# The second feed-forward matmul by Strassen's algorithm (seven half-block products for eight) in a fused hash-attention and feed-forward kernel

## The chip, the cores and the metric

One core of a Trainium2 chip. The metric is the device time of one execution in microseconds (us), smaller is better; it is quoted as the median of several executions, with the lowest and the highest. "Span" is the time that the profile of one execution shows; it is some 2 us less than the device time.

## The reference

```python
mask = q_bucket[:, :, :, None] == k_bucket[:, :, None, :]   # buckets from the signs of q @ proj, k @ proj (6 bits)
scores = np.where(mask, scale * q @ k.T, -1e9)
attn = softmax(scores)                                       # cut: with max and + 1e-9
x = (attn @ v)                                               # to (3072, 512)
h = x @ w_in                                                 # (3072, 2048)
g = h * (1 / (1 + exp(-h)))
out = g @ w_out                                              # (3072, 512)
```

Four batches of eight heads, 768 positions, 64 elements a head. A batch of attention yields 768 rows for the feed-forward part.

## The kernel before

The kernel goes through 288 steps, nine per head and 72 per batch. A step has one score matmul of 512 columns (two of 256 in every third step), one exp on ScalarE and four attention matmuls. Two heads are a "pair". While batch b is scored, TensorE works off "units" of the feed-forward part of batch b - 1, laid between the steps; a unit is 0.87 us of TensorE. What is left runs after the last score. Other work is planned by hand at fixed steps: the transposes of q and k (VectorE, L246), their casts (GpSimd, L251), the projection that yields the hash bits (L281), the loads.

The parts that the change touches; `ps` is the pool in PSUM. The tag "m" has three buffers, shared by h, the output sums, the projections and the transposes:

```python
        def mm1(ci, grp, dts=slice(0, NDT)):
            ... # cut
            hp = ps.tile([P, f, n], F32, tag="m", name="h_ps", bufs=3)
            ... # cut: 4 or 8 matmuls into hp (L461), tanh on ScalarE into th (L468)
            after.append(lambda: nc.vector.scalar_tensor_tensor(        # L470, frees hp
                out=g[ci][:, grp * f : (grp + 1) * f, :], in0=th, scalar=1.0, in1=hp,
                op0=ALU.add, op1=ALU.mult))

        def mm2(tt, part):
            ci, ct = (0, tt) if tt < 4 else (1, tt - 4)
            if part == 0:
                tag = "m" if scoring else "s"
                o2[tt] = ps.tile([P, DMODEL], F32, tag=tag, name="o2_ps", bufs=3)
            for ft in range(4 * part, 4 * part + 4):
                nc.tensor.matmul(o2[tt], g[ci][:, ft, ct * P : (ct + 1) * P],   # L496
                                 w_out16[:, ft, :],
                                 start=(ft == 0), stop=(ft == NFT - 1))
            if part == 3:
                ... # cut: eviction on VectorE (L501), output transfer
```

A row tile's sum takes four units of four matmuls and is then evicted once. Six row tiles a batch.

The softmax here doesn't subtract the row's maximum and nothing guards it: scores larger than these inputs give would overflow.

## Time and profile before

| | before |
|---|---|
| time, median of 3 | 303.24 us (303.05 to 303.79) |
| span of the profiled run | 301.3 us |
| granted TensorE clock | 1.0 |
| second matmul | 384 matmuls of 512 columns or their like |

The most telling views are in the prediction below. First VectorE's row in the 40 slices (each 7.5 us; a digit is the busy share in tenths): it has free time in most slices.

```profile
DVE  5797938899588355854694434954443443664332
```

Second, two stretches of steps (columns: from and to in us, length, then busy us and count of TensorE, weight loads, VectorE, ScalarE, GpSimd; then the clock, the DMA share and GB/s). The first is steps 96 to 126, the second steps 186 to 198:

```profile
69.60:94.00 24.40, 24.32 (x248) 15.54 (x246) 19.32 (x32) 20.78 (x40) 11.71 (x21) 1.00 0.99 168
148.20:159.20 11.00, 11.00 (x106) 6.93 (x105) 10.41 (x14) 8.70 (x17) 5.29 (x5) 1.00 0.60 107
```

TensorE fills both. In the second VectorE is already busy 10.41 of 11.00 us: there is no room there, and this was in plain sight before the change.

### The profile page before, as it was taken

The page shows a single profiled execution, that of the slowest core. Times are in us where ns is not written, and L with a number is a line of the kernel's source. Part 1 is how long each engine was busy: PE and PEld are TensorE (multiplying, and loading weights), DVE is VectorE, ACT ScalarE, POOL GpSimd, SP SyncE. Part 2 cuts the span into 40 slices and gives each one's busy share as a digit, 9 for nine tenths or more (in the row PEclk, how much of TensorE's full clock was granted, in tenths as well). Part 3 has the DMA queues.
Part 4 walks back from the last instruction along what each step waited for, and adds up shares of the span by engine and source line. Part 5 has one row for each costly group of instructions (what it writes and reads, how often), then busy time and mean ns, then how long its engine had stood idle before and what let it go on. Part 6 is the DMA issues. An engine that isn't in the chain of part 4 may idle for free.

```text
span 301.3 us, 7181 instructions
## 1 busy us (share of the span) xinstructions
PE 296.6 (98%) x2710; PEld 175.1 (58%) x2710; DVE 180.1 (60%) x344; ACT 210.1 (70%) x392; POOL 128.3 (43%) x203
## 2 busy tenths in 40 slices
PE   8999999999999999999999999999999999999996
PEld 3676855545665665555565665555566654446653
DVE  5797938899588355854694434954443443664332
ACT  5987989989886777778876666978977722452200
POOL 7589999388418551935158401755111100000000
PEclk9999999999999999999999999999999999999999
DMA  7999997999988638834078135011022003001112
GB/s 202 243 237 199 181 153 115 199 212 173 150 187 145 107 102 211 126 84 133 3 139 133 49 74 189 2 42 31 2 61 63 20 21 93 35 2 70 37 68 71
DMA packets 103170, 32.87 MB, mean 109 GB/s; under 512 B 90656, under 2 KB 100192, under 8 KB 103136
## 3 DMA queue, kind: packets, MB, share of 16 engines
q1 hardware_dynamic: 98752, 28.22, 44.6%
q0 software_dynamic: 4224, 4.19, 9.0%
q8 instruction: 21, 0.34, 0.5%
q14 instruction: 13, 0.11, 0.1%
q10 hardware_dynamic: 160, 0.00, 0.0%
HBM read 27.27 MB, written 6.29 MB: 111 GB/s over the span
## 4 chain that ended last, share of the span: by engine, by line
PE 88%; DVE 7%; DMA 1%; ACT 1%; issue 1%; SPq 1%; DVEq 0%; ACTq 0%
PE o_ps L496 26%; PE h_ps L461 24%; PE s_ps L366 19%; PE o_ps L398 12%; DVE g L470 3%; PE bp_ps L281 3%; PE tp_ps L185 2%; DMA k_row<-in_k_dram 1%; PE o_ps L482 1%; DVE qk L246 1%; DVE qka L343 1%; ACT u L369 1%; DVE osum L412 1%; SPq L79 0%; PE o_ps L389 0%
## 5 line engine op out<-in xcount | busy, mean ns | idle before, releaser
L369 ACT ACTIVATE u<-s_ps 128x512 f16<-128x512 f32 x288 | 157.0, 606 | 38.7 <-PE s_ps L366 38.3
L470 DVE SCALAR_TENSOR_TENSOR g<-th,h_ps 128x512 f16<-128x512 f32 x96 | 65.5, 687 | 73.8 <-ACT th L468 73.8
L461 PE MATMUL h_ps<-xT,win 128*128 128x512 f16 (+1 forms) x512 | 98.4, 325 | 0.1
L398 PEld LDWEIGHTS <-u 128*128 128x128 f16 x1152 | 68.1, 98 | 42.2 <-ACT u L369 8.4
L496 PE MATMUL o_ps<-wout,g 128*128 128x512 f16 x368 | 91.6, 379 | 0.0
L398 PE MATMUL o_ps<-vv,u 128*128 128x65 f16 x1152 | 82.6, 194 | 0.5 <-ACT u L369 0.4
L468 ACT ACTIVATE th<-h_ps 128x512 f32<-128x512 f32 x96 | 57.9, 603 | 35.9 <-PE h_ps L461 33.2
L461 PEld LDWEIGHTS <-win 128*128 128x128 f16 x512 | 49.9, 98 | 30.5 <-issue 0.4
L418 POOL TENSOR_TENSOR x_pr<-osum,rec 128x384 f16<-128x384 f32 x23 | 19.0, 826 | 88.5 <-DVE rec L417 88.0
L496 PEld LDWEIGHTS <-g 128*128 128x128 f16 x368 | 35.8, 98 | 33.7
L366 PE MATMUL s_ps<-qka 71*128 71x512 f16 x192 | 52.7, 327 | 0.0
L366 PE MATMUL s_ps<-qkb 128*128 128x512 f16 x192 | 52.6, 326 | 0.0
L251 POOL TENSOR_SCALAR qka<-qk 64x1536 f16<-64x1536 f32 x15 | 22.0, 1466 | 11.5 <-DVE qk L246 5.7
L501 DVE TENSOR_SCALAR osb<-o_ps 128x512 f32<-128x512 f32 x23 | 15.9, 691 | 15.0 <-PE o_ps L496 15.0
L251 POOL TENSOR_SCALAR qkb<-qk 64x1536 f16<-64x1536 f32 x15 | 22.1, 1471 | 1.2
L262 POOL TENSOR_TENSOR vsa<-v_sb 128x192 f32<-128x192 f32 x32 | 18.9, 591 | 0.0
L260 POOL CAST vv<-v_sb 128x384 f16<-128x384 f32 x32 | 16.2, 507 | 1.0 <-DMA v_sb<-in_v_dram 0.6
L246 DVE STREAM_TRANSPOSE qk<-k_blk 128x768 f32<-128x768 f32 x10 | 15.8, 1582 | 0.3 <-issue 0.3
L246 DVE STREAM_TRANSPOSE qk<-q_blk 128x768 f32<-128x768 f32 x10 | 16.0, 1596 | 0.0
L366 PEld LDWEIGHTS <-qka 71*128 71x128 f16 x192 | 15.5, 97 | 0.4 <-ACT qka L238 0.3
L366 PEld LDWEIGHTS <-qkb 128*128 128x128 f16 x192 | 15.4, 97 | 0.0
L412 DVE TENSOR_TENSOR osum<-o_ps,vsum 128x390 f32<-128x390 f32 x23 | 13.0, 565 | 2.3
(70 smaller groups left out, 162.5 us busy)
## 6 DMA issues: line engine op xcount, KB each, us to landing
out_dram<-osb SPq DMA_DIRECT2D x23, 256.0 KB
v_sb<-in_v_dram SPq DMA_DIRECT2D x15, 384.0 KB
q_blk<-in_q_dram SPq DMA_DIRECT2D x40, 96.0 KB
k_blk<-in_k_dram SPq DMA_DIRECT2D x40, 96.0 KB
win<-in_moe_w_in_dram POOLq DMA_DIRECT2D x4, 512.0 KB, 7.7
wout<-in_moe_w_out_dram POOLq DMA_DIRECT2D x4, 512.0 KB, 6.2
q_sb<-in_q_dram SPq DMA_DIRECT2D x5, 384.0 KB
k_sb<-in_k_dram SPq DMA_DIRECT2D x5, 384.0 KB
```

What stands on the lines that cost most here:

```text
L246: nc.vector.transpose(out=dst, in_=qk_sb[p, "qk"[n]])
L251: nc.gpsimd.tensor_scalar(out=dst[rows, :], in0=qk32[p][rows, :], scalar1=CS, scalar2=1.0, op0=ALU.mult, op1=ALU.mult)
L260: nc.gpsimd.tensor_copy(out=vv[:, :, 0:D], in_=src)
L262: nc.gpsimd.tensor_tensor(out=sa, in0=src[:, 0:3], in1=src[:, 3:6], op=ALU.add)
L366: nc.tensor.matmul(sp[:, o0 : o0 + n], t[rows, S + jt * P : S + (jt + 1) * P], t[rows, c0 : c0 + n], start=True, stop=True)
L369: nc.scalar.activation(out=u, in_=sp, func=AF.Exp, scale=ESC)
L398: nc.tensor.matmul(o_ps[h][:, c0 // P + i, :], u[:, o0 + i * P : o0 + (i + 1) * P], vv[:, jt, :], start=(not direct(h) and w % NU == 0 and ...
L418: (nc.vector if direct(h) else nc.gpsimd).tensor_tensor(out=x_pr[p][:, :, par * D : (par + 1) * D], in0=o[:, 0:NJ, 0:D], in1=rec[:, :, Non ...
L461: nc.tensor.matmul(hp[:, j, :], w_in16[:, dt, ft * P : (ft + 1) * P], xT[4 * b + dt][:, c0 : c0 + n], start=(dt == 0), stop=(dt == NDT - 1))
L468: nc.scalar.activation(out=th, in_=hp, func=AF.Tanh, scale=0.5)
L470: after.append(lambda: nc.vector.scalar_tensor_tensor(out=g[ci][:, grp * f : (grp + 1) * f, :], in0=th, scalar=1.0, in1=hp, op0=ALU.add, o ...
L496: nc.tensor.matmul(o2[tt], g[ci][:, ft, ct * P : (ct + 1) * P], w_out16[:, ft, :], start=(ft == 0), stop=(ft == NFT - 1))
```

## The change

Intent: TensorE is the bound, so multiply less. The matrix product of one chunk of rows is cut into 2 x 2 blocks and done by Strassen's algorithm in Winograd's form, with seven block products for eight. The seven share PSUM sums so that few extra additions are needed. VectorE makes the combinations of the blocks of g (for each chunk) and of w_out (once), in float16. The core of the diff:

```diff
-    ld = ...bufs=4  vld = ...bufs=4  t32 = ...bufs=3          # shortened here: three pools
+    ld = ...bufs=3  vld = ...bufs=3  t32 = ...bufs=2
+    def w_unit(n, half):                                       # planned at steps 96 to 110, 1024 elements each
+        f = slice(half * NK // 2, (half + 1) * NK // 2)
+        dst, x, y = {1: (wt[1], B12, B11), 2: (wt[2], B22, wt[1]),
+                     3: (B12, B22, B12), 4: (wt[4], B21, wt[2])}[n]
+        nc.vector.tensor_tensor(out=dst[:, f], in0=x[:, f], in1=y[:, f], op=ALU.subtract)
...
-        def mm2(tt, part):                                     # and mm2_last: removed
+        def comb(ci, n, f):                                    # cut: choice of blocks
+            nc.vector.tensor_tensor(out=dst, in0=x, in1=y, op=op)
...
+        def product(ci, n, t):
+            nt = 2 - ci
+            bank, x, y = {1: (1, (0, 0), B11), 2: (1, (1, 0), B21),
+                          6: (2, (0, 0), wt[2]), 5: (2, (0, 1), wt[1]), 3: (2, (1, 0), B22),
+                          7: (3, None, B12), 4: (3, (1, 1), wt[4])}[n]
+            ... # cut: a product opens its bank for n in 1, 6, 7
+            for k in range(NK):
+                nc.tensor.matmul(op[:, t, :], x[:, k, t * P : (t + 1) * P], y[:, k],
+                                 start=(first and k == 0), stop=True, skip_group_check=True)
+            ... # cut
+            add = {1: None, 2: None, 6: 1, 5: 1, 3: 1, 7: 5, 4: 6}[n]
+            keep = n in (1, 6, 5)                              # a copy in the middle of a sum
+            ... # cut: eviction of op, plus kept[add], scaled by 0.5; output transfer unless keep
...
+        units = spread(first[:-3], late) if late else first[:-3]
+        units = units + [big[0]] + first[-3:] + [big[1]] + spread(second, big[2:8])
+        late[:] = big[8:] + small
...
-            skip = w * 36 // 66 == (w - 1) * 36 // 66
+            skip = w * 32 // 66 == (w - 1) * 32 // 66
...
+    last += [late[i] for i in (6, 0, 1, 7, 8, 2, 3, 9, 4, 10, 11, 5, 12)]
```

Line numbers in the changed kernel: L474 first matmul, L524 product, L378 score, L410 attention matmul, L293 projection, L486 g, L507 combination of g, L186 combination of w_out, L534 eviction, L536 eviction with an addition, L258 block transpose of q and k, L263 cast.

More of the change, by code (lines that the diff above doesn't have):

```diff
@@ L47 @@
     cst = ctx.enter_context(tc.tile_pool(name="cst", bufs=1))
-    ld = ctx.enter_context(tc.tile_pool(name="ld", bufs=4))
-    vld = ctx.enter_context(tc.tile_pool(name="vld", bufs=4))
-    t32 = ctx.enter_context(tc.tile_pool(name="t32", bufs=3))
+    ld = ctx.enter_context(tc.tile_pool(name="ld", bufs=3))
+    vld = ctx.enter_context(tc.tile_pool(name="vld", bufs=3))
+    t32 = ctx.enter_context(tc.tile_pool(name="t32", bufs=2))
     btp = ctx.enter_context(tc.tile_pool(name="btp", bufs=2))
@@ L163 @@
     w_out16 = cst.tile([P, NFT, DMODEL], F16, name="wout")
+    NK = NFT // 2
+    NC = DMODEL // 2
+    wt = {n: cst.tile([P, NK, NC], F16, name=f"wt{n}") for n in (1, 2, 4)}
+    B11, B12 = w_out16[:, 0:NK, 0:NC], w_out16[:, 0:NK, NC:DMODEL]
+    B21, B22 = w_out16[:, NK:NFT, 0:NC], w_out16[:, NK:NFT, NC:DMODEL]
     def load_w_in(i):
@@ L444, in moe_units @@
     def moe_units(b):
-        g = {}
+        blk = {}
         opened = {}
@@ L451, in mm1 @@
             c0, n, f = ((0, 512, 1), (512, 256, 2))[ci]
-            if ci not in g:
-                g[ci] = gpl.tile([P, NFT, n], F16, tag=f"g{ci}", name="g",
-                                 bufs=2 - ci)
+            ft0 = grp * f
+            half = ft0 // NK
+            if (ci, half) not in blk:
+                blk[ci, half] = gpl.tile([P, 2, NK, n // 2], F16, tag=f"g{ci}{half}", name="g",
+                                         bufs=2 if (ci, half) == (0, 1) else 1)
             hp = opened.pop((ci, grp), None)
             if dts.start == 0:
-                hp = ps.tile([P, f, n], F32, tag="m", name="h_ps", bufs=3)
+                hp = ps.tile([P, 2, f, n // 2], F32, tag="m", name="h_ps", bufs=3)
             for j in range(f):
-                ft = grp * f + j
+                ft = ft0 + j
                 for dt in range(dts.start, dts.stop):
-                    nc.tensor.matmul(hp[:, j, :], w_in16[:, dt, ft * P : (ft + 1) * P],
-                                     xT[4 * b + dt][:, c0 : c0 + n],
+                    nc.tensor.matmul(hp[:, :, j, :], w_in16[:, dt, ft * P : (ft + 1) * P],
+                                     xT[4 * b + dt][:, c0 : c0 + n]
+                                     .rearrange("d (r c) -> d r c", r=2),
                                      start=(dt == 0), stop=(dt == NDT - 1))
@@ L466, in mm1 @@
                 return
-            th = thp.tile([P, f, n], F32, tag="th", name="th")
+            th = thp.tile([P, 2, f, n // 2], F32, tag="th", name="th")
             nc.scalar.activation(out=th, in_=hp, func=AF.Tanh, scale=0.5)
-            after.append(lambda: nc.vector.scalar_tensor_tensor(
-                out=g[ci][:, grp * f : (grp + 1) * f, :], in0=th, scalar=1.0, in1=hp,
-                op0=ALU.add, op1=ALU.mult))
-        o2 = {}
-        def mm2_last():
-            for c in (slice(0, 384), slice(384, DMODEL)):
-                n = c.stop - c.start
-                op = ps.tile([P, n], F32, tag="s", name="o2_ps", bufs=3)
-                for ft in range(NFT):
-                    nc.tensor.matmul(op, g[1][:, ft, P : 2 * P], w_out16[:, ft, c],
-                                     start=(ft == 0), stop=(ft == NFT - 1))
-                osb = ops.tile([P, n], F32, tag="osb", name="osb")
-                nc.vector.tensor_scalar(out=osb, in0=op, scalar1=0.5, scalar2=None,
-                                        op0=ALU.mult)
-                dst = out[b * S : (b + 1) * S, c].rearrange("(p t) n -> p t n", p=P)
-                nc.sync.dma_start(out=dst[:, NJ - 1, :], in_=osb)
@@ L490, in mm2, with g_op @@
-        def mm2(tt, part):
-            ci, ct = (0, tt) if tt < 4 else (1, tt - 4)
-            if part == 0:
-                tag = "m" if scoring else "s"
-                o2[tt] = ps.tile([P, DMODEL], F32, tag=tag, name="o2_ps", bufs=3)
-            for ft in range(4 * part, 4 * part + 4):
-                nc.tensor.matmul(o2[tt], g[ci][:, ft, ct * P : (ct + 1) * P],
-                                 w_out16[:, ft, :],
-                                 start=(ft == 0), stop=(ft == NFT - 1))
-            if part == 3:
-                osb = ops.tile([P, DMODEL], F32, tag="osb", name="osb")
-                nc.vector.tensor_scalar(out=osb, in0=o2[tt], scalar1=0.5, scalar2=None,
-                                        op0=ALU.mult)
-                dst = out[b * S : (b + 1) * S, :].rearrange("(p t) n -> p t n", p=P)
-                nc.sync.dma_start(out=dst[:, tt, :], in_=osb)
+            def g_op():
+                k0 = ft0 % NK
+                nc.vector.scalar_tensor_tensor(
+                    out=blk[ci, half][:, :, k0 : k0 + f, :].rearrange("p r f c -> p r (f c)"),
+                    in0=th.rearrange("p r f c -> p r (f c)"), scalar=1.0,
+                    in1=hp.rearrange("p r f c -> p r (f c)"),
+                    op0=ALU.add, op1=ALU.mult)
@@ new lines, in mm1 @@
+            after.append(g_op)
+        def comb(ci, n, f):
+            if n == 3 and (ci, 3) not in blk:
+                w = blk[ci, 0].shape[-1]
+                blk[ci, 3] = gpl.tile([P, NK, w], F16, tag=f"g{ci}d", name="gd", bufs=1)
+            a11, a21 = blk[ci, 0][:, 0, f], blk[ci, 0][:, 1, f]
+            a12, a22 = blk[ci, 1][:, 0, f], blk[ci, 1][:, 1, f]
+            dst, x, y, op = {3: (blk.get((ci, 3)), a11, a21, ALU.subtract),
+                             1: (a21, a21, a22, ALU.add),
+                             2: (a11, a21, a11, ALU.subtract),
+                             4: (a12, a12, a11, ALU.subtract)}[n]
+            if n == 3:
+                dst = dst[:, f]
+            nc.vector.tensor_tensor(out=dst, in0=x, in1=y, op=op)
@@ new lines, in moe_units @@
+        banks, kept = {}, {}
+        def product(ci, n, t):
[3 more added lines that the diff above has]
+                          7: (3, None, B12), 4: (3, (1, 1), wt[4])}[n]
+            x = blk[ci, 3] if x is None else blk[ci, x[0]][:, x[1]]
+            first = t == 0 and n in (1, 6, 7)
+            if first:
+                banks[ci, bank] = ps.tile([P, nt, NC], F32, tag="m" if scoring else "s",
+                                          name="o2_ps", bufs=3)
+            op = banks[ci, bank]
+            for k in range(NK):
+                nc.tensor.matmul(op[:, t, :], x[:, k, t * P : (t + 1) * P], y[:, k],
+                                 start=(first and k == 0), stop=True, skip_group_check=True)
+            if t < nt - 1:
+                return
+            add = {1: None, 2: None, 6: 1, 5: 1, 3: 1, 7: 5, 4: 6}[n]
+            keep = n in (1, 6, 5)
+            pool = nrm if keep else ops
+            o = pool.tile([P, nt, NC], F32, tag=f"part{ci}{n}" if keep else "osb", name="osb",
+                          bufs=1 if keep else 3)
+            if add is None:
+                nc.vector.tensor_scalar(out=o, in0=op, scalar1=0.5, scalar2=None, op0=ALU.mult)
+            else:
+                nc.vector.scalar_tensor_tensor(out=o, in0=op, scalar=0.5, in1=kept[ci, add],
+                                               op0=ALU.mult, op1=ALU.add)
+            if keep:
+                kept[ci, n] = o
+                return
+            r, c = {2: (0, 0), 3: (0, 1), 7: (1, 1), 4: (1, 0)}[n]
+            t0 = 4 * ci + r * nt
+            dst = out[b * S : (b + 1) * S, c * NC : (c + 1) * NC].rearrange(
+                "(p t) n -> p t n", p=P)
+            nc.sync.dma_start(out=dst[:, t0 : t0 + nt, :], in_=o)
@@ L506, in moe_units, with then, unit @@
+        def then(fn, *combs):
+            def unit():
+                fn()
+                for c in combs:
+                    after.append(lambda c=c: comb(*c))
+            return unit
+        lo, hi, al = slice(0, NK // 2), slice(NK // 2, NK), slice(0, NK)
         first = [lambda grp=grp: mm1(0, grp) for grp in range(NFT)]
+        for grp, c in ((9, (0, 3, lo)), (11, (0, 3, hi)), (13, (0, 1, lo)), (15, (0, 1, hi))):
+            first[grp] = then(first[grp], c)
         second = [lambda grp=grp: mm1(1, grp) for grp in range(NFT // 2)]
-        outs = {tt: [lambda tt=tt, part=part: mm2(tt, part) for part in range(4)]
-                for tt in range(NJ)}
@@ L510, in moe_units @@
-        if b == B - 1:
-            outs[NJ - 1] = [mm2_last]
+        for grp, c in ((0, (0, 2, hi)), (5, (1, 3, al)), (7, (1, 1, al))):
+            second[grp] = then(second[grp], c)
+        big = [lambda n=n, t=t: product(0, n, t) for n in (1, 2, 6, 5, 3, 7, 4) for t in range(2)]
+        for i, c in ((1, (0, 2, lo)), (3, (0, 4, lo)), (5, (0, 4, hi))):
+            big[i] = then(big[i], c)
+        small = [lambda n=n: product(1, n, 0) for n in (1, 2, 6, 5, 3, 7, 4)]
+        for i, c in ((0, (1, 2, al)), (1, (1, 4, al))):
+            small[i] = then(small[i], c)
@@ L515, in moe_units, with spread @@
             first = one[0] + one[1] + one[2] + one[3] + first[2:]
-        return first, second, outs
-    def spread(x, y):
+        return first, second, big, small
+    def spread(x, y, at=None):
         both = [((i + 0.5) / len(x), 0, u) for i, u in enumerate(x)]
@@ L530, in moe_list @@
     def moe_list(b):
-        first, second, outs = moe_units(b) if b else first_units
-        units = spread(first, late) + spread(second, outs[0] + outs[1] + outs[2])
-        late[:] = outs[3] + outs[4] + outs[5]
+        first, second, big, small = moe_units(b) if b else first_units
+        units = spread(first[:-3], late) if late else first[:-3]
+        units = units + [big[0]] + first[-3:] + [big[1]] + spread(second, big[2:8])
+        late[:] = big[8:] + small
         return units
@@ L627 @@
                 plan(w0 + (28 if Q == 3 else 8) + i, lambda p=2 * Q + 2 + i: load_blocks(p))
+    for i, n in enumerate((1, 2, 3, 4)):
+        for half in range(2):
+            plan(96 + 4 * i + 2 * half, lambda n=n, half=half: w_unit(n, half))
     for p in range(NPAIR):
@@ L670 @@
     scoring = False
-    for u in moe_head() + moe_list(B - 1) + late:
+    last = moe_head() + moe_list(B - 1)
+    last += [late[i] for i in (6, 0, 1, 7, 8, 2, 3, 9, 4, 10, 11, 5, 12)]
+    for u in last:
         u()
```

## The prediction

The 0.68 us of a combination can be worked out from the rows of the float16 copies alone: 384 more elements took 200 ns, which leaves 345 - 200 = 145 ns fixed, and 1024 x 200 / 384 + 145 = 678 ns (an estimate). The 109.2 and 215.8 ns of a matmul are distances of starts, 109.1 to 109.3 and 215.9 to 216.2 ns in the mean of such streams in the trace of the kernel before. The second rival's time assumed a slower rate of the combinations that no row shows (the chance tied to it: 0.04 for more than 309.3 us).

> **What bounds the kernel now.** I read the summary of busy time first, then the chain that ended last, then the table by stretches, then the order of time on TensorE and VectorE in two stretches, and last the groups by shape for the price of one instruction.
>
> The summary and the chain: TensorE is busy for nearly all of the span, its clock is granted in full, and 88% of the chain runs through it. The second matmul (o_ps at L496) is the largest part.
>
> ```profile
> PE 296.6 (98%) x2710; PEld 175.1 (58%) x2710; DVE 180.1 (60%) x344; ACT 210.1 (70%) x392; POOL 128.3 (43%) x203
> ...
> PEclk9999999999999999999999999999999999999999
> ...
> PE 88%; DVE 7%; DMA 1%; ACT 1%; issue 1%; SPq 1%; DVEq 0%; ACTq 0%
> PE o_ps L496 26%; PE h_ps L461 24%; PE s_ps L366 19%; PE o_ps L398 12%; DVE g L470 3%; PE bp_ps L281 3%; PE tp_ps L185 2%; DMA k_row<-in_k_dram 1%; PE o_ps L482 1%; DVE qk L246 1%; DVE qka L343 1%; ACT u L369 1%; DVE osum L412 1%; SPq L79 0%; PE o_ps L389 0%
> ```
>
> By stretches (columns: us, then busy us and count of TensorE, weight loads, VectorE, ScalarE, GpSimd). From 92 us on TensorE has no gap, so time cut from its stream there is time won. VectorE is different from stretch to stretch: 17.7 of 22.5 us at 69.5 to 92, only 25 of 58 at the end.
>
> ```profile
> 69.50:92.00 22.50, 22.43 (x225) 14.39 (x223) 17.66 (x30) 19.60 (x38) 10.78 (x20) 1.00 1.01 173
> 92.00:109.70 17.70, 17.63 (x187) 11.06 (x186) 8.78 (x16) 12.71 (x25) 11.97 (x21) 1.00 0.60 111
> 142.60:179.10 36.50, 36.50 (x350) 22.80 (x349) 21.22 (x35) 26.61 (x49) 15.74 (x24) 1.00 0.42 79
> 243.70:301.30 57.60, 54.80 (x310) 29.16 (x307) 25.17 (x39) 15.53 (x26) 0.00 (x0) 1.00 0.14 50
> ```
>
> The order of time on TensorE near the end (start, us, line): durations overlap, so the price is the distance of the starts. Eight matmuls of 256 columns take 287.07 - 286.20 = 0.87 us, 109 ns each; 36 of 512 columns take 294.84 - 287.07 = 7.77 us, 215.8 ns each. The width can be halved at almost no loss.
>
> ```profile
> 286.20 1.04 PE L461 MATMUL h_ps<-xT,win 128*128 128x256 f16 x8
> 287.07 7.93 PE L496 MATMUL o_ps<-wout,g 128*128 128x512 f16 x36
> 294.84 3.66 PE L482 MATMUL o_ps<-wout,g 128*128 128x384 f16 x32
> ```
>
> VectorE's prices (count, busy us, mean ns): g and an eviction of 512 columns cost 0.69 us each, a dense run of them some 0.6 start to start. The last two rows are the only float16 work from SBUF to SBUF: 384 more elements cost 200 ns[...].
>
> ```profile
> L470 DVE SCALAR_TENSOR_TENSOR g<-th,h_ps 128x512 f16<-128x512 f32 x96 | 65.5, 687 | 73.8 <-ACT th L468 73.8
> L501 DVE TENSOR_SCALAR osb<-o_ps 128x512 f32<-128x512 f32 x23 | 15.9, 691 | 15.0 <-PE o_ps L496 15.0
> L343 DVE COPY qka<-bits 13x768 f16<-13x768 f16 x12 | 6.5, 545 | 0.2
> L320 DVE COPY qka<-bits 13x384 f16<-13x384 f16 x4 | 1.4, 345 | 0.1
> ```
>
> [...]
>
> **The change part by part.** Per batch the second matmul was 96 matmuls of 512 columns, 96 x 215.8 = 20.7 us. Now it is seven products of 8 k-tiles on three row tiles, 7 x 8 x 3 = 168 matmuls of 256 columns, 168 x 109.2 = 18.35 us. That removes 2.37 us a batch, 9.5 us in four: 3.1% of 303.24, the most that can be had. The first matmul keeps its counts and its columns; only the place of its results changes.
>
> VectorE gains 12 combinations of g per batch and 8 of w_out once, each 1024 float16 elements: 56 x 0.68 = 38 us. Evictions go from six of 512 columns a batch (4.1 us) to seven of 512 and seven of 256 (0.69 and, between the trace's 0.29 for 128 and 0.56 for 384, 0.42 us): 7.8 us, 3.6 more a batch, 14.5 in all. VectorE rises from 180 to about 233 us, 78% of the span. On average it fits. ScalarE and GpSimd keep their work. The output goes out in about as many, narrower transfers, on queues with room. The smaller pools (4 to 3, 4 to 3, 3 to 2 buffers) matter little: in the order of instructions nearly every load or transpose that now waits for a buffer waits for a reader planned many steps earlier; the worst waits for one planned in the same step.
>
> What comes back as waiting on TensorE, worked out from the order of the changed instructions with the durations above:
>
> First batch, w_out combined. In the 30 steps from 96 to 125 (69.5 to 92 us before) there are 15 combinations, 10.2 us, and one more eviction, on top of 17.7 us: 28.6 us, less some 2.4 for dense running, 26. TensorE has some 21 there with its slower pace of units. Three PSUM buffers for h and the sums hold off 1.5 to 2 us. So 3.3 us of waiting (1.5 to 6), as first-matmul units waiting for a PSUM buffer.
>
> Second batch around the first eviction: in steps 189 to 196 VectorE has three block transposes (3 x 1.42 spaced), three g, three combinations and the eviction, some 9.3 us against 6.8 us of TensorE work; I find about 1.0 us. The third batch has no block transposes there: 0.3.
>
> At the heads of the second and third batch, product 4 follows product 7 in the same bank, whose eviction stands behind a block transpose: 0.25 us each, 0.5.
>
> After the scores, where nothing else fills TensorE. Product 7 to product 4, directly one after the other: 0.2 to the start of the eviction, 0.69, and its semaphore: 0.95 us. Last batch, product 2 after product 1: two units lie between (1.74 us), while VectorE must do g (start 0.95 after its matmul), a combination, then the eviction: 3.1 us, so 1.4 us. In the reordered last 13 products the same count leaves 0.35 us, and the last eviction and its 256-column transfer end perhaps 0.3 later. Together 3.0, of which I take 2.6.
>
> Sum: -9.5 + 3.3 + 1.3 + 0.5 + 2.6 = -1.8 us, that is 301.4; the waits partly hide each other, so I say 301.2.
>
> **The rivals.** First: all of the waiting is hidden and the change is worth its 9.5 us, 293.8. For it speaks that VectorE stands idle 73.8 us before g alone and that the schedule has clearly been laid out by hand with distances between the products. Against it: this idle time lies in other stretches than the new work, and a bank that has to be copied out in mid-sum is a wait that did not exist. Half hidden would be 297. Second: VectorE becomes the bound. [...] Third: the combinations collide with GpSimd, busy 11 of 22.5 us in the dense stretch. A combination held for part of a 1.47 us cast would add some 0.2 us to each, 3 us in the dense stretch alone: 303 to 305. [...] Fourth: the narrow matmuls are held up by weight loads (98 ns mean against 109 ns spacing). The 256-column rows above keep 109 ns with a new weight tile each time, so I give this little.
>
> **Range and chances.** With the waits at half their sum the time is 297.5; with the collisions at full, 304.5. So 297.7 to 304.5. Faster than 297.2, the 2% line, needs waits under 3.4 us in all: 0.12. [...] Within: 0.84.
>
> **What would show each step.** The second matmul should have 672 matmuls of 256 columns, start to start 109 ns, whatever comes of the time. The combinations should read about 680 ns, VectorE's busy time about 230 us. TensorE should show gaps around 69 to 95 us, before products 2 and 4, and about 1.4 us once after 260 us. If [...]TensorE is gapless, or GpSimd's readers run longer, one of the rivals is right. I am wrong if the time is under 297: then the buffers hide more than I count.

## The result

| | before | changed |
|---|---|---|
| time, median of 4 | 303.51 us (303.05 to 303.88) | 310.61 us (310.38 to 310.73) |
| span | 301.3 us | 308.6 us |
| ratio | | 1.023, 95% interval 1.0203 to 1.0258 |

Ratios here and below are the mean time of one kernel's runs over that of the other's in the same rounds, so not quite the ratio of the medians. The result is correct and slower by 2.3%; 301.2 was predicted, with 304.5 as the upper end.

The changed kernel's summary, the rows that changed, and the chain that ended last:

```profile
PE 294.3 (95%) x2982; PEld 203.3 (66%) x2982; DVE 230.3 (75%) x431; ACT 209.3 (68%) x392; POOL 134.5 (44%) x203
...
DVE  5687848899999655975799666984757564778772
...
PEclk9999999999689999999999999999999999999999
...
PE 69%; DVE 18%; DMA 4%; ACT 3%; SPq 2%; issue 2%; DVEq 0%; ACTq 0%
```

TensorE is 95% busy instead of 98%, and VectorE's part of the chain has gone from 7% to 18%. VectorE's row has a run of nines where the combinations of w_out fall. The granted clock dips in the two slices between 77 and 93 us.

The second matmul and the combinations by shape (count, busy us, mean ns of one):

```profile
L524 PE MATMUL o_ps<-wt,g 128*128 128x256 f16 x288 | 36.9, 272 | 1.3 <-DVE osb L536 1.0
L524 PE MATMUL o_ps<-wout,g 128*128 128x256 f16 x288 | 36.7, 272 | 3.1 <-DVE osb L534 2.5 <-DVE g L486 0.3 <-DVE osb L536 0.3
L507 DVE TENSOR_TENSOR g<-g 128x1024 f16<-128x1024 f16 x36 | 29.3, 814 | 0.3
L507 DVE TENSOR_TENSOR gd<-g 128x1024 f16<-128x1024 f16 x12 | 8.8, 736 | 0.0
```

The 672 narrow matmuls (288 + 288, and 96 on gd) are there, at 109 ns start to start, as predicted. So the saving on TensorE is real: 384 x 215.8 ns = 82.9 us has become 672 x 109.2 ns = 73.4 us, 9.5 us less. The combinations read 736 to 814 ns in the mean, where 680 was predicted.

Where the time went, by steps (the kernel cut at the first attention matmul of a step, lengths in us; the last four columns are experiments told below):

| steps | before | changed | no combinations, no copies in mid-sum | best correct version | short fills | long fills |
|---|---|---|---|---|---|---|
| start to 96 | 69.5 | 69.1 | 69.1 | 69.6 | 69.1 | 69.1 |
| 96 to 126 | 24.4 | 29.5 | 23.4 | 25.5 | 26.5 | 29.6 |
| 126 to 160 | 30.0 | 30.5 | 29.7 | 30.0 | 30.5 | 30.6 |
| 160 to 186 | 24.3 | 24.5 | 24.4 | 24.6 | 24.4 | 24.4 |
| 186 to 216 | 30.9 | 31.4 | 28.9 | 31.7 | 29.3 | 29.8 |
| 216 to 287 | 64.6 | 63.5 | 63.3 | 62.2 | 63.3 | 63.3 |
| 287 to the end | 57.6 | 60.0 | 58.4 | 57.4 | 59.9 | 60.2 |
| span | 301.3 | 308.6 | 297.2 | 300.9 | 303.0 | 307.0 |

The loss stands in two rows: +5.1 us in steps 96 to 126, and +2.4 us after the last score. The two stretches shown above for the kernel before, and the row after the scores, read in the changed kernel:

```profile
69.10:98.60 29.50, 26.84 (x260) 18.06 (x259) 28.87 (x46) 21.75 (x41) 15.12 (x21) 0.88 0.98 149
153.60:166.80 13.20, 11.38 (x118) 8.09 (x117) 12.87 (x16) 9.18 (x18) 4.29 (x4) 1.00 0.95 164
248.60:308.60 60.00, 54.22 (x428) 41.37 (x428) 39.59 (x68) 15.52 (x26) 0.00 (x0) 1.00 0.16 52
```

In the first, VectorE is busy 28.87 of 29.50 us, in the second 12.87 of 13.20. In both VectorE sets the pace now, and TensorE has gaps. In the third it has plenty of time (39.6 of 60 us), so what is lost there is order, not load.

The waits that are new (engine, line, what for: us in total, times, longest):

```profile
PEld bp_ps L293 <- DVE g L486: 4.0, 3, 1.6
PE h_ps L474 <- DVE g L486: 2.7, 3, 1.8
PE o_ps L524 <- DVE osb L534: 2.5, 2, 1.4
PE o_ps L524 <- DVE osb L536: 1.3, 3, 0.8
```

In the kernel before the list of waits has only this one of them, about half as long:

```profile
PEld bp_ps L281 <- DVE g L470: 2.1, 4, 1.0
```

"h_ps waits for g" is the full PSUM pool: a unit of the first matmul needs the buffer that the g of three tiles earlier frees. "o_ps waits for osb" is the bank that must be copied out in the middle of its sum. The order of time on TensorE in the dense stretch:

```profile
78.53 1.02 PE L474 MATMUL h_ps<-xT,win 128*128 128x512 f16 x4 [1.84 <-DVE g L486]
...
81.18 1.87 PE L474 MATMUL h_ps<-xT,win 128*128 128x512 f16 x4 [0.48 <-DVE g L486]
...
84.14 1.91 PE L474 MATMUL h_ps<-xT,win 128*128 128x512 f16 x4
85.84 0.42 PE L410 MATMUL o_ps<-vv,u 128*128 128x65 f16 x4
```

TensorE stands for 1.84 us and 0.48 us. Between these two gaps its clock falls to half, and stays there from 79.6 to 86.4 us: the unit at 84.14 takes 1.70 us to the next start instead of 0.87. My first reading was that the halved clock costs some 3 us. It does not: the four runs of the changed kernel had granted clocks of 0.988, 0.989, 1.0 and 1.0, and took 310.38, 310.56, 310.73 and 310.66 us. The runs with the full clock are no faster. While VectorE sets the pace, a slower TensorE cost nothing here. Whether the clock falls differed between runs of one kernel: in this profile it fell 1.1 us after the end of the gap of 1.84 us; in run 4 the profiled execution of the long fills has a wait of 2.0 us at a clock of 0.998, and two of the other three had 0.989.

VectorE, then GpSimd, shortly before product 1 of the second batch is copied out (start, us):

```profile
158.67 1.75 DVE L507 TENSOR_TENSOR g<-g 128x1024 f16<-128x1024 f16 x1
...
163.07 0.69 DVE L507 TENSOR_TENSOR g<-g 128x1024 f16<-128x1024 f16 x1
```

```profile
158.42 1.46 POOL L263 TENSOR_SCALAR qka<-qk 64x1536 f16<-64x1536 f32 x1 [0.87 <-DVE qk L258]
159.96 1.79 POOL L263 TENSOR_SCALAR qkb<-qk 64x1536 f16<-64x1536 f32 x1
```

The combination at 158.67 starts during a cast and takes 1.75 us, ending 0.54 us after the cast does (158.42 + 1.46 = 159.88 against 160.42); the next cast is stretched to 1.79 in its turn. The one at 163.07, with no cast beside it, takes 0.69. So the collisions of the prediction's third rival are there; all 17 combinations of more than 0.70 us ended 0.54 to 0.55 us after the end of a GpSimd instruction that they met. Over all 56 combinations the durations sum to 44.6 us, where 56 undisturbed ones would be 56 x 0.684 = 38.3: the collisions added 6.3 us of VectorE time. Whether they cost as much on the clock, the experiments must tell.

### The profile page after: what moved, and what is told of

Read it like the earlier page. It is cut to its first block, busy times and chain, and to the rows that moved or that the text cites. A ratio compares the mean times of both kernels' runs of the same rounds, so it can differ in the third digit from the quotient of the medians.

```text
span 308.6 us, 7844 instructions
## 1 busy us (share of the span) xinstructions
PE 294.3 (95%) x2982; PEld 203.3 (66%) x2982; DVE 230.3 (75%) x431; ACT 209.3 (68%) x392; POOL 134.5 (44%) x203
## 4 chain that ended last, share of the span: by engine, by line
PE 69%; DVE 18%; DMA 4%; ACT 3%; SPq 2%; issue 2%; DVEq 0%; ACTq 0%
PE o_ps L524 20%; PE h_ps L474 19%; PE s_ps L378 15%; PE o_ps L410 9%; DVE g L486 5%; DVE qk L258 2%; PE bp_ps L293 2%; PE tp_ps L197 2%; DVE g L507 2%; SPq L92 1%; DMA q_blk<-in_q_dram 1%; DMA k_blk<-in_k_dram 1%; DVE wt L186 1%; ACT th L482 1%; ACT u L381 1%
## 5 line engine op out<-in xcount | busy, mean ns | idle before, releaser
L474 PE MATMUL h_ps<-xT,win 128*128 128x512 f16 (+1 forms) x512 | 100.2, 329 | 2.8 <-DVE g L486 2.7
L486 DVE SCALAR_TENSOR_TENSOR g<-th,h_ps 128x512 f16<-128x512 f32 x96 | 65.0, 682 | 41.8 <-ACT th L482 40.9
L410 PEld LDWEIGHTS <-u 128*128 128x128 f16 x1152 | 68.5, 98 | 33.1 <-ACT u L381 9.6
L410 PE MATMUL o_ps<-vv,u 128*128 128x65 f16 x1152 | 83.2, 194 | 1.2 <-ACT u L381 1.0
L474 PEld LDWEIGHTS <-win 128*128 128x128 f16 x512 | 50.1, 98 | 31.7 <-issue 6.3
L524 PEld LDWEIGHTS <-g 128*128 128x128 f16 x576 | 56.2, 98 | 18.1 <-issue 6.1
L430 POOL TENSOR_TENSOR x_pr<-osum,rec 128x384 f16<-128x384 f32 x23 | 19.9, 867 | 80.4 <-DVE rec L429 80.0
L378 PE MATMUL s_ps<-qka 71*128 71x512 f16 x192 | 53.7, 332 | 0.0
L378 PE MATMUL s_ps<-qkb 128*128 128x512 f16 x192 | 52.5, 326 | 0.0
L524 PE MATMUL o_ps<-wout,g 128*128 128x256 f16 x288 | 36.7, 272 | 3.1 <-DVE osb L534 2.5
L524 PE MATMUL o_ps<-wt,g 128*128 128x256 f16 x288 | 36.9, 272 | 1.3 <-DVE osb L536 1.0
L263 POOL TENSOR_SCALAR qka<-qk 64x1536 f16<-64x1536 f32 x15 | 21.9, 1462 | 20.5 <-DVE qk L258 12.6
L536 DVE SCALAR_TENSOR_TENSOR osb<-o_ps,osb 128x512 f32<-128x512 f32 (+1 forms) x40 | 22.1, 552 | 10.9 <-PE o_ps L524 10.8
L507 DVE TENSOR_TENSOR g<-g 128x1024 f16<-128x1024 f16 x36 | 29.3, 814 | 0.3
L263 POOL TENSOR_SCALAR qkb<-qk 64x1536 f16<-64x1536 f32 x15 | 22.7, 1512 | 1.2
L274 POOL TENSOR_TENSOR vsa<-v_sb 128x192 f32<-128x192 f32 x32 | 20.2, 630 | 0.0
L272 POOL CAST vv<-v_sb 128x384 f16<-128x384 f32 x32 | 17.1, 534 | 1.0 <-DMA v_sb<-in_v_dram 0.6
L378 PEld LDWEIGHTS <-qka 71*128 71x128 f16 x192 | 15.7, 98 | 0.4 <-issue 0.2
L258 DVE STREAM_TRANSPOSE qk<-k_blk 128x768 f32<-128x768 f32 x10 | 15.8, 1582 | 0.0
L258 DVE STREAM_TRANSPOSE qk<-q_blk 128x768 f32<-128x768 f32 x10 | 15.8, 1578 | 0.0
```

What stands on the lines that cost most here:

```text
L258: nc.vector.transpose(out=dst, in_=qk_sb[p, "qk"[n]])
L263: nc.gpsimd.tensor_scalar(out=dst[rows, :], in0=qk32[p][rows, :], scalar1=CS, scalar2=1.0, op0=ALU.mult, op1=ALU.mult)
L274: nc.gpsimd.tensor_tensor(out=sa, in0=src[:, 0:3], in1=src[:, 3:6], op=ALU.add)
L378: nc.tensor.matmul(sp[:, o0 : o0 + n], t[rows, S + jt * P : S + (jt + 1) * P], t[rows, c0 : c0 + n], start=True, stop=True)
L410: nc.tensor.matmul(o_ps[h][:, c0 // P + i, :], u[:, o0 + i * P : o0 + (i + 1) * P], vv[:, jt, :], start=(not direct(h) and w % NU == 0 and ...
L474: nc.tensor.matmul(hp[:, :, j, :], w_in16[:, dt, ft * P : (ft + 1) * P], xT[4 * b + dt][:, c0 : c0 + n] .rearrange("d (r c) -> d r c", r=2 ...
```

## The experiments

The load theory: VectorE's plain work in the two dense stretches, together with the copies in mid-sum, is what costs. The collision theory (its rival): the meeting of the two-input combinations with GpSimd. A third: one of the quieter parts of the change, the halved width or the smaller pools. The sections are numbered, and "run 3" below means the run of section 3.

### 1. Narrow matmuls alone, and smaller pools alone

The kernel before with each matmul of 512 columns done as two of 256, correct:

```diff
-                nc.tensor.matmul(o2[tt], g[ci][:, ft, ct * P : (ct + 1) * P], w_out16[:, ft, :], ...)
+                for c in (slice(0, 256), slice(256, 512)):
+                    nc.tensor.matmul(o2[tt][:, c], g[ci][:, ft, ct * P : (ct + 1) * P], w_out16[:, ft, c], ...)
```

> The kernel before with each matmul of the second product cut into two of 256 columns, each with its own weight load, nothing else changed (right result). If width costs only 2 x 109.2 - 215.8 = 2.6 ns a pair: 384 x 2.6 ns = 1.0 us more, 304.5 us. If weight loads hold the narrow matmuls up: 307 us or more.

Measured: 304.40 us (303.90 to 304.96) against 303.41; ratio 1.0034 (1.0011 to 1.0058). One microsecond, as 384 x (2 x 109.2 - 215.8) ns = 1.0 us says. The narrow shape is no culprit.

The kernel before with the smaller pools, correct:

```diff
-    ld bufs=4, vld bufs=4, t32 bufs=3
+    ld bufs=3, vld bufs=3, t32 bufs=2
```

> The kernel before with only the smaller pools of the change (loads 3 for 4, values 3 for 4, transposed q and k 2 for 3; right result). If the smaller pools matter little, as the prediction said: 302.5 to 304.5 us. If they hold the loads up so that pair 8's bits land late: 305 us or more, with a wait of the scores near 110 us.

Measured: 303.54 us (303.40 to 304.52) against 303.44; ratio 1.0009 (0.9989 to 1.0030). No cost. The third theory falls in both parts.

### 2. No combinations at all

The result is wrong: `comb` and `w_unit` return at once, and the products read the uncombined blocks. Everything else stays, the copies in mid-sum too.

```diff
         def comb(ci, n, f):
+            return
...
     def w_unit(n, half):
+        return
```

> All 56 combinations of g and w_out taken out (wrong result on purpose), the seven products, their mid-sum copies and the evictions kept. If VectorE's combinations are what TensorE waits for, nearly all of the 16 us of added gaps go and only the mid-sum bank waits stay (0.95 us after the scores, some 0.4 us in the last products): 296 to 298.5 us. If the mid-sum copies or the narrow matmuls cost the time, little is gained: 305 us or more.

Measured: 303.25 us (302.00 to 305.75) against 303.41; ratio 1.0001 (0.9946 to 1.0055). 7.4 us better than the changed kernel, so the combinations are the seat of the loss; but the load theory had asked for more: 303.25 lies between the two expectations. The trace shows why: with VectorE out of the way, another wait came out. On TensorE:

```profile
106.67 0.28 PE L410 MATMUL o_ps<-vv,u 128*128 128x65 f16 x4
109.56 0.59 PE L378 MATMUL s_ps<-qka 71*128 71x512 f16 x1 [2.61 <-DMA qka<-bits]
```

The hash bits of pair 8 come by DMA, and the queue that issues it:

```profile
100.70 2.65 SPq L92 DMA_DIRECT2D k_blk<-in_k_dram  x4
103.45 2.29 SPq L445 DMA_TRANSPOSE xT<-x_pr  x1
105.83 0.53 SPq L545 DMA_DIRECT2D out_dram<-osb  x1
106.47 1.74 SPq L343 DMA_DIRECT2D qka<-bits  x2
```

Four issues of a load take 2.65 us, 0.66 each. In this queue the issues stand in the order of the program, and the sixteen loads of pairs 10 and 11 stand ahead of the bits. These were issued at 106.47 us, just when TensorE wanted them; in the kernel before it was 101.64 us, 6.3 us ahead of their use at 107.93:

```profile
101.64 1.72 SPq L331 DMA_DIRECT2D qka<-bits  x2
```

Around the end of this gap the clock is halved here too, from 109.4 to 116.2 us (0.62 in the mean from 108 to 114 us; the expectation of run 3 says some 4 us), and this time the time goes with it: the four runs with clocks of 0.989, 0.994, 0.998 and 1.0 took 305.75, 304.16, 302.00 and 302.35 us. There is no VectorE bound for it to hide behind (VectorE is busy 1.17 of the 6.00 us from 108 to 114); but whether the wait itself was as long in the fast runs is not on record.

### 3. The same, with the loads of pairs 10 and 11 planned later

```diff
-                plan(w0 + (28 if Q == 3 else 8) + i, lambda p=2 * Q + 2 + i: load_blocks(p))
+                plan(w0 + {3: 28, 4: 21}.get(Q, 8) + i, lambda p=2 * Q + 2 + i: load_blocks(p))
```

> As the run without combinations, and the loads of pairs 10 and 11 issued from step 129 on instead of 116, after pair 8's bits (wrong result on purpose). There, one wait of 2.8 us of pair 8's scores for its bits stood at 106.8 us, with half clock for some 4 us after it. If that was the queue of the loads, both go: 297 to 300 us. If the waits only move elsewhere: 302 us or more.

Measured: 300.77 us (300.43 to 302.06) against 303.44; ratio 0.9919 (0.9894 to 0.9944), between the two expectations. The wait for the bits is gone. Steps 96 to 126 fell from the changed kernel's 29.5 us to 23.4, gapless on TensorE:

```profile
69.10:92.50 23.40, 23.40 (x264) 17.08 (x263) 19.46 (x32) 21.22 (x41) 12.09 (x21) 1.00 1.01 157
```

So 6.1 us of that stretch come with the combinations (run 2, with the loads where they were, has 23.4 us there too). What remains is 0.55 us at 152 us, 1.55 us at 117 us (the first matmul of the second batch waiting for xT, which now stands behind the moved loads in the same queue), and the waits after the scores.

### 4. Load or collision: combinations replaced by fills

Wrong. Each combination becomes a memset, which reads nothing from SBUF, so that VectorE stays busy; that the fills do not collide was assumed, and their rows below show none (685 ns in the mean of 36). The first version fills 600 elements of g (558 ns) and 512 of w_out (485 ns); the second 752 and 768 elements, 685 and 698 ns, rows as long as that of an undisturbed combination.

```diff
-            nc.vector.tensor_tensor(out=dst, in0=x, in1=y, op=op)
+            nc.vector.memset(m[:, 0:600], 0.5)          # second version: 0:752
```

> Each combination replaced by a memset of about the same length (600 or 512 elements [...]) that reads nothing from SBUF (wrong result on purpose). Theory of collisions with GpSimd: the combinations' excess of 6.3 us over 56 x 0.684 us is what tips the first batches over, so 303 to 305 us. Theory of plain load on VectorE: only a third of the loss or less is undone, 306 to 309 us.

> As the run with memsets, but 752 elements long, which by the two lengths measured there (485 ns for 512, 558 for 600) is some 0.68 us, as long as an undisturbed combination (wrong result on purpose). So only the collisions with GpSimd are taken away. If the collisions are what tips it over: 304.5 to 307 us. If shorter work did it in the first such run: 308 us or more.

Measured: the short fills 304.77 us (304.56 to 305.49) against 303.41, ratio 1.0045 (1.0024 to 1.0065); the long ones 308.76 us (308.72 to 309.72) against 303.44, ratio 1.0184 (1.0161 to 1.0207). In the long version GpSimd's casts are as in the kernel before (1471 ns there), and the rows of the fills are as long as those of undisturbed combinations:

```profile
L509 DVE MEMSET g<- 128x752 f16 x36 | 24.7, 685 | 3.8
L264 POOL TENSOR_SCALAR qkb<-qk 64x1536 f16<-64x1536 f32 x15 | 22.0, 1469 | 1.2
```

(In the changed kernel the same casts have 1512 ns, by the collisions.) By the rows alone the long version would be the fair one, and collisions would be worth 310.61 - 308.76 = 1.9 us. But the rows hide how long VectorE is held. An undisturbed combination of the changed kernel between two other instructions, then a long fill:

```profile
163.68 0.68 DVE L534 TENSOR_SCALAR osb<-o_ps 128x512 f32<-128x512 f32 x1
164.28 0.68 DVE L507 TENSOR_TENSOR g<-g 128x1024 f16<-128x1024 f16 x1
164.88 1.56 DVE L258 STREAM_TRANSPOSE qk<-k_blk 128x768 f32<-128x768 f32 x1
```

```profile
87.19 0.63 DVE L487 SCALAR_TENSOR_TENSOR g<-th,h_ps 128x512 f16<-128x512 f32 x1
87.92 0.69 DVE L509 MEMSET g<- 128x752 f16 x1
88.52 0.63 DVE L536 TENSOR_SCALAR osb<-o_ps 128x512 f32<-128x512 f32 x1
```

The combination starts 0.08 us before the instruction ahead of it ends, the fill 0.10 us after. In a dense run the two starts around a combination lie 1.20 us apart (164.88 - 163.68), those around a long fill 1.33 to 1.39, around a short one of g 1.18 to 1.23, around a short one of w_out 1.08. With the earlier end of the instruction behind a fill taken off, a long fill holds VectorE some 0.135 us longer than a combination, a short one of g some 0.02 us less, one of w_out 0.12 us less. So the long version has more plain load than the changed kernel (by 56 x 0.135 = 7.6 us of VectorE), and the short one less (by 48 x 0.02 + 8 x 0.12 = 1.9 us). They are bounds: the collisions are worth between 1.9 us and 310.61 - 304.77 = 5.8 us. The long version is four times as far off as the short one. A straight line between the two times puts the collisions at some 5 us of the 7.1 us loss; the same line, drawn for the two stretches below, puts them at some 4 (estimates). Of the two expectations for the long version the second came true, 308 or more, yet not for its reason. Steps 96 to 126 of the short version, then of the long one:

```profile
69.10:95.60 26.50, 24.11 (x260) 17.02 (x259) 24.93 (x46) 21.36 (x41) 12.15 (x21) 1.00 1.00 155
69.10:98.60 29.50, 24.37 (x260) 16.94 (x259) 27.29 (x46) 21.38 (x41) 12.12 (x21) 1.00 1.04 159
```

The line between them gives 27.6 us without collisions: of the 6.1 us that the combinations cost here (29.5 against 23.4), some 4.2 are load and 1.9 collisions, which had stretched the combinations by 2.0 us. In steps 186 to 216 it gives 29.4: of 2.5 us some 0.5 are load and 2.0 collisions. So both theories hold, each in another stretch for the larger part. The split is an estimate; a fill that holds VectorE exactly as long as a combination was not run. The products also read other blocks in these two kernels, so a part of what is put down to collisions may be waits for a combination.

### 5. Moving the combinations of w_out

Correct. Half of them go behind step 126:

```diff
-    for i, n in enumerate((1, 2, 3, 4)):
-        for half in range(2):
-            plan(96 + 4 * i + 2 * half, lambda n=n, half=half: w_unit(n, half))
+    for w, n, half in ((98, 1, 0), (102, 1, 1), (105, 2, 0), (109, 2, 1),
+                       (126, 3, 0), (129, 3, 1), (134, 4, 0), (137, 4, 1)):
+        plan(w, lambda n=n, half=half: w_unit(n, half))
```

> The eight combinations of w_out moved: w1 and w2 to steps 98 to 109, w3 and w4 to steps 126 to 137, after the dense stretch and still before their first use (right result). If the first batch's loss is VectorE's crowding at steps 96 to 112, the 3.4 us of gaps near 74 to 81 us and the drop of the clock after them (some 3 us) go in large part: 304 to 306 us and the clock stays full. If the loss is spread over all batches: 309 us or more.

Measured: 310.08 us (308.59 to 311.23) against 303.41; ratio 1.0213 (1.0176 to 1.0249). Almost nothing in the end: the second expectation. Steps 96 to 126 fell from 29.5 to 26.1 us, but steps 126 to 160 rose from 30.5 to 32.3: the projection of pairs 8 and 9 then waited 2.3 us for VectorE. The run at the full clock took 308.59, the three at 0.994 took 310.05 to 311.23, so some 1.5 us of the gain seem to go to the clock.

### 6. Order of units, places of loads and combinations together

Correct. Four edits: the combinations of w_out at steps 102 to 110 and 127 to 137; the loads of pairs 10 and 11 at 129 and 130; the products laid so that more units lie between a product and the next one in its bank; the units of the last 24 steps paced evenly, so that some are left for the last attention matmuls.

```diff
-        units = units + [big[0]] + first[-3:] + [big[1]] + spread(second, big[2:8])
-        late[:] = big[8:] + small
+        units = units + first[-3:-1] + big[:2] + [first[-1], second[0], second[1], big[2], second[2], ...]  # cut
+        late[:] = big[8:12] + [small[0]] + big[12:] + small[1:]
...
+        if w >= NW - 24:
+            e = w - (NW - 24)
+            n = (e + 1) * ending // 24 - e * ending // 24
...
-    last += [late[i] for i in (6, 0, 1, 7, 8, 2, 3, 9, 4, 10, 11, 5, 12)]
+    last += [late[i] for i in (4, 0, 1, 7, 8, 2, 3, 9, 5, 10, 11, 6, 12)]
```

> A right kernel with the waits attacked by order alone: w_out's combinations spread, loads of pairs 10 and 11 after pair 8's bits, product 1 finished before the last first-matmul units, two or three units between a mid-sum copy and the next product in its bank, even pace in the last 24 steps. If the gaps are a matter of distance: the tail's 4.1 us of gaps fall to about 1, the 1.6 us of the second batch go, some of the first batch's stay: 301 to 305 us. If VectorE's load sets the time anyway: 308 us or more.

Measured: 303.70 us (303.40 to 304.63) against 303.44; ratio 1.0013 (0.9992 to 1.0034). 6.9 us less than the changed kernel, with the same instructions in another order. The gaps after the scores sum to about 0.6 us (4.0 in the changed kernel). It left a wait of 1.9 us at 122 us for xT, behind the moved loads in SyncE's queue, so I split these: pair 10 back to step 116, pair 11 to step 147.

```diff
-                plan(w0 + {3: 28, 4: 21}.get(Q, 8) + i, ...)
+                plan(w0 + (28 + i if Q == 3 else 8 + 31 * i if Q == 4 else 8 + i), ...)
```

> The reordered correct kernel with one more edit: the eight load transfers of pair 10 go back to step 116 and those of pair 11 move to step 147, so that neither stands ahead of pair 8's bits nor ahead of the xT transposes of pairs 6 and 7 in the DMA queue. If that queue is the reason for the 1.9 us in which the first matmul of batch 1 waited for xT at 121.9 to 124 us, this wait falls below 0.4 us and the time is 301.4 to 302.3 (ratio about 0.995). If the wait has another reason (VectorE late with x), it stays and the time is 303.4 to 304.

Measured: 302.98 us (302.58 to 303.75) against 303.64; ratio 0.9982 (0.9964 to 1.0000). The wait for xT is gone (steps 126 to 160 from 31.9 to 30.0 us), so the queue was its reason; the median fell by 0.7 us, less than the expected 1.4 or more, while the profiled span fell by 2.0. Most of the difference is the choice of the profiled run: of the first kernel the slowest of four was profiled (304.63 us, 0.9 above the median), of the second one 0.3 below the median. So the 1.9 us of waiting are those of a slow run. This is the best correct version: the same as the kernel before within what can be told, perhaps 0.2% better. Its dense stretch:

```profile
69.50:95.00 25.50, 23.99 (x260) 16.99 (x259) 24.87 (x42) 21.82 (x42) 14.67 (x21) 1.00 1.03 160
```

VectorE is busy 24.87 of 25.50 us: it still sets the pace there.

One more edit on top moved the block transposes of pairs 12 and 13 five steps forward, to take them out of steps 186 to 198:

```diff
-            w1 = w0 + (5, 9, 12, 15)[i]
+            w1 = w0 + ((0, 3, 7, 10) if Q == 6 else (5, 9, 12, 15))[i]
```

> The kernel before this one with the four block transposes of pairs 12 and 13 moved from steps 185, 189, 192, 195 to 180, 183, 187, 190: no less work for VectorE, only earlier. If the 1.65 us gap at 160 us (first-matmul units waiting for a buffer) and the 1.6 us in the projection at 166 us come from block transposes, combinations and the first eviction falling into the same 8 steps, about 2 us of the 3.2 go: 299.5 to 300.3. If VectorE is simply full over the whole stretch of steps 180 to 198, the wait moves to an earlier step and the time stays within 0.5 us of the kernel without the move.

Measured: 303.38 us (302.40 to 304.91) against 303.64; ratio 0.9994 (0.9969 to 1.0020). No gain. The three runs with a clock of 0.998 or more took 302.40 to 302.88 us, the three at 0.993 to 0.994 took 303.88 to 304.91. The waits at the projection shrank from 1.6 to 0.3 us beyond their usual spacing, but the unit at 159 us then waited 2.4 us instead of 1.6, and two smaller waits of 0.2 and 0.4 came ahead of it. This is the second of the two expectations, that VectorE is full over the whole stretch. It is not the only reading: in steps 186 to 216 the combinations were stretched by 2.9 us in this run and by 1.9 in the one before it, so the move also brought more collisions, and the two were not told apart.

### 7. What the saved TensorE work is worth when nothing is given back

Wrong: no combinations, and no copies in mid-sum either; pair 11's load at step 147.

```diff
+            if keep:
+                return
+            add = None
```

> Wrong result on purpose: no combinations at all, and also no copies in the middle of a sum (three per row half and batch, 24 in all); pair 11's load at step 147. Only the 672 narrow matmuls and the final evictions remain, so this is what the saved TensorE work is worth when nothing is given back. If the saving of 9.5 us is there to be had: 293.5 to 296, the gaps between product 7 and product 4 and before product 2 gone, and the first-matmul gap at 117 us too. If something else in the changed order of units holds TensorE, it stays above 298. The difference to the run without combinations alone (300.8), less about 1.5 for the moved load, is the price of the copies in mid-sum: I expect 3 to 4.

Measured: 298.55 us (298.24 to 298.96) against 303.64; ratio 0.9833 (0.9815 to 0.9852). The expectation of 293.5 to 296 was missed: with nothing given back, the time falls by 5.1 us, and the span by 4.1, not 9.5. The distances between the starts of TensorE's instructions, summed by kind and compared with the kernel before, say what became of the rest: the narrow matmuls are 9.6 us shorter; against it stand, with smaller ones, 0.95 between product 7 and product 4, 0.8 in the last attention matmuls (no units left beside them), 1.1 after score matmuls, 1.1 after projection matmuls, and 1.2 at the end, from the last matmul to the end of the span (3.06 us before, 4.28 here):

```profile
245.94 0.27 PE L524 MATMUL o_ps<-wout,g 128*128 128x256 f16 x1 [0.78 <-DVE osb L537]
...
293.21 0.42 DVE L537 TENSOR_SCALAR osb<-o_ps 128x256 f32<-128x256 f32 x1 [0.18 <-PE o_ps L524]
```

```profile
298.54 0.29 DVE L485 TENSOR_SCALAR osb<-o_ps 128x128 f32<-128x128 f32 x1 [0.34 <-PE o_ps L482]
```

The first fence is this run: product 4 waits for the eviction of product 7 even here, and the last eviction has 256 columns. The second fence is the kernel before, which had cut its last tile so that the last eviction has 128 columns. The step from run 3 to this one, 2.2 us, was to be 1.5 for the load and 3 to 4 for the copies; the copies in mid-sum are thus worth 0.7 us or so by themselves, less than I thought (0.8 by the table's last stretch, 59.2 us in run 3 and 58.4 here).

## Why the prediction was wrong

The waits that come back were put at 7.5 us and measured 308.6 - (301.3 - 9.5) = 16.8. Of the 9.3 us between, some 4.1 stay on TensorE without any combination and were not named, and some 4 to 5 (an estimate) are collisions, which were named as a rival and left out of the sum. By its own steps:

- **The saving, -9.5 us.** Right on TensorE: 672 matmuls, 109 ns, and run 1 shows the price of the narrow shape. As a saving of time it was taken in full, with the waits set against it. Run 7 shows that only 4.1 us of span come out even with VectorE's new work gone, so this term failed as well. The 5.4 us in between are waits that stay; of these the prediction named the 0.95 between products 7 and 4 and 0.3 for the last eviction, and not the last attention matmuls or the projections. Part of them is shown to lie in the order of the units: from step 216 to the end run 6, with another order and all the combinations, takes 119.6 us and run 7 takes 121.7. The cause of the rest is open.
- **VectorE's load.** Right in its sum: 230.3 us busy, "about 233" predicted; an undisturbed combination takes 0.68 us to the digit.
- **First batch, 3.3 us. This is the step that failed in the mechanism.** It had VectorE at 28.6 us in steps 96 to 125, took off 2.4 for dense running to get 26, set TensorE against it at 21, and let three buffers hold off 1.5 to 2. The 2.4 was not the fault: VectorE's instructions there sum to 31.4 us and keep it busy for 29.0. Three things were not. The stretch was read too short: step 125 of the kernel before ends at 93.9 us, not at 92, so VectorE starts from 19.3 us, not 17.7, and TensorE's own work is 23.4 us (run 3), not 21. The buffers held off nothing: VectorE was busy 28.87 of 29.5 us, and TensorE had all of the difference as waits. And the collisions were left out. The term measured 29.5 - 23.4 = 6.1 us, of which some 4.2 are load and 1.9 collisions by the estimate of run 4, and 0.8 more in the steps behind it (30.5 against 29.7 in the table).
- **Second and third batch, 1.3 us.** 31.4 - 28.9 = 2.5 us in steps 186 to 216, where VectorE had 0.6 us free in 11 before the change. Product 2 behind the eviction of product 1 and the projection behind it both waited. Without collisions it is 0.4 to 0.9 us (29.3 and 29.8 in run 4), within the 1.0 that the prediction counted; the other 1.6 to 2.1 is its third rival, which it left out of the sum. The third batch, without block transposes, was right to be small: 0.2 us in steps 216 to 287.
- **The heads of the batches, 0.5 us.** One gap of 0.27 us at 191 us, and 0.15 in steps 160 to 186: small, as said, and hardly there.
- **After the scores, 2.6 us.** The gaps sum to 4.0. The two that it named are there: 0.95 between products 7 and 4 (0.95 predicted), and 1.2 before product 2 (1.4 predicted). The waiting product 2, and the eviction which ends just before it:

```profile
281.08 0.68 DVE L534 TENSOR_SCALAR osb<-o_ps 128x512 f32<-128x512 f32 x1
```

```profile
281.82 1.03 PE L524 MATMUL o_ps<-wout,g 128*128 128x256 f16 x8 [1.05 <-DVE osb L534]
```

  It missed 0.8 in the last attention matmuls and two of 0.43 us between products; the end of the span is 0.6 us later instead of 0.3.
- **The rivals.** The third (collisions, some 0.2 us each, 3 us in the dense stretch) was named and left out of the sum. It came true (6.3 us of VectorE time over 56, 0.11 each): run 4 puts it between 1.9 and 5.8 us over the whole kernel, 4 to 5 by estimate, about half of it in the second batch, where the prediction had not looked for it. The fourth, weight loads, was rightly given little. The second, "VectorE becomes the bound", was tied to a slower rate of the combinations and dismissed with it; it came true without that rate, in two stretches: steps 96 to 126, where VectorE was busy for 19.3 of 24.4 us before, and 186 to 198, where it was nearly full already.
- **"The waits partly hide each other".** No run shows that they did. It was not tested apart: the losses of the table are parts of one span and add up in any case.

In one line of spans: 301.3 - 9.5 + 5.4 (what stays in run 7) + 6.9 (steps 96 to 160) + 2.5 (steps 186 to 216) + 1.6 (the combinations and copies after the scores, 60.0 - 58.4) + 0.4 (the rest of the table) = 308.6. Run 6 takes back 6.9 to 7.6 us of time by order and places alone; no run here made VectorE's load itself smaller in a correct kernel.

What stays open: how much of the 1.9 us wait for xT the typical run of run 6's first kernel has; what causes the waits of run 7 that run 6 does not take back; and whether a version with fewer block transposes on VectorE would keep more of the saving.

## What to carry to other kernels

When work moves from the bounding engine to one that is "60% busy", compare the two engines in each stretch in which the new work falls, not over the span: here VectorE was 95% busy in one of the stretches before the change, and with the new work that stretch became nearly as long as VectorE's busy time (13.2 against 12.87 us). A test that takes away a suspected interference must keep the time for which the engine is held, from start to start of the neighbours; the same length of the row is not enough (0.685 us for both here, and 0.135 us more in truth), and two tests on either side give bounds. And a halved clock in the profile is not yet a cause: compare runs with and without it. Here, where VectorE set the pace, it was free: 310.38 and 310.56 us with it, 310.73 and 310.66 without.
